# DeltaNet and mixture of depths on one core: TensorE filler products, two of six block inversions on GpSimd, the others in PSUM, `y` in one bank

## The chip, the cores and the metric

The kernel runs on one core of a Trainium2 chip. The time is the device time of one execution in microseconds (us); lower is better. Three runs of the kernel before took 437.75, 440.28 and 440.36 us, median 440.28.

Five engines work in their own instruction order and wait for one another through semaphores: TensorE (PE in the profile; PEld is its weight loading), VectorE (DVE), ScalarE (ACT), GpSimd (POOL) and SyncE (SP), which here only issues DMAs. SBUF is the working memory with 128 partitions, PSUM the memory into which TensorE writes.

## The reference

Two parts follow each other. The first is a DeltaNet recurrence over 768 tokens for 4 batches of 8 heads with head size 48; the second picks 128 of 768 tokens of each batch by a score, sends them through a two-layer MLP and adds the gated result.

```python
k_n = k / (np.linalg.norm(k, axis=-1, keepdims=True) + 1e-06)
for t in range(S):
    y[:, :, t] = np.einsum('bhd,bhde->bhe', q[:, :, t], state)
    v_old = np.einsum('bhde,bhd->bhe', state, kt)
    state = state + bt[:, :, :, None] * np.einsum('bhd,bhe->bhde', kt, vt - v_old)
...
scores = np.einsum('bsd,d->bs', x, w_gate)     # x is y with the heads side by side
for b in range(B):
    top_idx = np.argpartition(-scores[b], capacity)[:capacity]
    xe = x[b, top_idx]
    ye = np.maximum(xe @ w1, 0.0) @ w2
    out[b, top_idx] = x[b, top_idx] + g[:, None] * ye      # g: sigmoid of the score
```

## The kernel before

**Units and blocks.** The recurrence is done in chunks of 64 tokens. Two batches with all their heads (16 sequences) make a group, and a chunk of a group is a unit: 2 groups x 12 chunks = 24 units, `i` = 0 to 23, each group's 12 one after the other because the state passes from chunk to chunk. Within a chunk the tokens depend on each other through a triangular 64x64 system. The kernel inverts its two 32x32 diagonal halves directly and joins them with products. Four units make a block, `e` = 0 to 5, whose 32x32 triangles stand side by side on VectorE's 128 partitions.

**Preparation (`prep`, L383).** For each unit SP loads `k` and `q`; TensorE transposes them (L335) into PSUM banks of the ring `inv`, ScalarE copies them to `kq` (L339); TensorE forms `k k` and `k q` products (L352), ScalarE copies them to `g` and `p` (L361); GpSimd masks `p` with two selects (L369); two DMAs in SP's queue shift half of `g` to other columns (L380).

**Elimination (`eliminate`, L418).** Once per block on VectorE: transpose `g` into `a` (L423), norms and scales (L433 to L438; the root on ScalarE), GpSimd makes the table `mb` (L441), scale (L448), then 30 steps of two instructions each. Step `j` multiplies column `j` of the rows below with row `j` into `tmp` (L458) and subtracts that from the rows below (L462), so that (31 - j) x j elements per partition are worked on twice; both operands are in SBUF. Then the table (L468) and two transposes back (L471 into `tt`, L476 into `g`); SP moves half of `tt` (L482).

**Join (`join`, L500).** For each unit two sets of 32 small 32x32 products (L514, L525) with ScalarE's copies between (L519, L530). The first set waits for L471.

**Recurrence (`recur`, L540).** For each unit a chain: products of `k` with the state (L562), VectorE's subtraction from `v` (L566), products with the inverse (L574), two copies on ScalarE (L580), the update of the state in PSUM (L588, weights from `k`), a copy of it (L594), and on to the next unit. Beside the chain stand VectorE's scaling of `v` (L554) and the output `y`: products of `q` with the state (L601) and of `p` (L611). Two units share a PSUM tile `py` of two banks, each writing one half of its partitions. Every second unit ScalarE copies `y` to `x` (L618), SP stores it (L626), VectorE forms the score (L632).

**Depths (`depths`, L677).** For each of 4 batches: the scores are spread over all partitions (L687 on GpSimd, L697 on TensorE), VectorE counts each token's rank (L729, L734), makes the selection (L742), TensorE turns it into indices (L749), GpSimd gathers 128 rows (L764), TensorE runs the MLP (L770, L780, L794), ScalarE gates (L799), GpSimd adds the rows to the output (L803).

**Order of the work.** All instructions are written out by a planner (`Plan`, L26). Each piece of work has an engine, a reckoned duration, dependences and a due time (`prio`, lower first). The planner runs through time, always takes the piece that can start first, on equal start the lower due time, and emits them in order of their planned starts; every engine works through its own list in that order. Rings (`ring`, L202) are sets of buffers; a piece that takes one waits in the plan until one is free. `k` has 10 buffers, `kq` and `p` have 9 each, so nine units can be prepared ahead, `g` and `tt` have 2 (blocks), `inv` has 3 PSUM banks, `y` one tile of two banks, and `prec` and `psta` take the other three banks.

## Time and profile before

| | us |
|---|---|
| median of 3 runs | 440.28 |
| the profiled execution | 440.75 |
| its span, first to last instruction | 439.0 |
| TensorE busy (PE) | 325.6 |
| VectorE busy | 279.6 |
| ScalarE busy | 154.5 |
| GpSimd busy | 65.0 |
| mean granted clock of TensorE | 0.754 |

[...] "Busy" for TensorE is the time in which at least one matmul was under way. An engine that waits is listed with the instruction that released it. A duration stands for one instruction unless a count (x32) follows; then it is the time of all of them together.

### The profile page before, as it was taken

Reading aid. Unit: us, or ns where it says so; the run is one execution under the profiler, and the core shown is the slowest. Engines: PE = TensorE matmul, PEld = TensorE weight load, DVE = VectorE, ACT = ScalarE, POOL = GpSimd, SP = SyncE. Lnnn points to the kernel's source line nnn. Section 1 sums busy time; section 2 is a strip of 40 time slices with the busy share of each in tenths; the row PEclk is TensorE's granted clock in tenths of the full one; section 3 lists DMA queues with packets and bytes.
Section 4 is the critical chain, followed back from the end, with each engine's and each line's share of the span. In section 5 each row is a group of like instructions: output and inputs, shape, how many; then the busy total and the mean of one; then the engine's idle time right before and its main releaser. Section 6 shows DMA issues by size and latency. Waiting matters only on the chain. (4 is left out here: it accounts for less than half of the span.)

```text
span 439.0 us, 13687 instructions
## 1 busy us (share of the span) xinstructions
PE 325.6 (74%) x5884; PEld 282.2 (64%) x5884; DVE 279.6 (64%) x741; ACT 154.5 (35%) x381; POOL 65.0 (15%) x84
## 2 busy tenths in 40 slices
PE   2749508996999849996999608999429999339383
PEld 2637308994898749875898408997329997128281
DVE  3029999689748997699655998469995110984000
ACT  0545405346534633546423605342016141201010
POOL 3025212014011212023010310100100001100201
PEclk9965755798559965998559955599855699757869
DMA  9545764355325541354223202222111011100201
GB/s 124 106 86 102 143 187 106 60 121 92 82 37 116 111 81 31 84 108 88 55 40 75 37 6 45 55 56 38 19 25 40 19 40 18 37 18 1 35 1 18
DMA packets 108444, 27.92 MB, mean 64 GB/s; under 512 B 103072, under 2 KB 107808, under 8 KB 108384
## 3 DMA queue, kind: packets, MB, share of 16 engines
q1 hardware_dynamic: 103184, 24.67, 27.0%
q0 software_dynamic: 832, 1.57, 2.2%
q10 hardware_dynamic: 4368, 0.80, 1.3%
q8 instruction: 46, 0.75, 0.7%
q14 instruction: 14, 0.11, 0.1%
HBM read 18.38 MB, written 5.51 MB: 54 GB/s over the span
## 5 line engine op out<-in xcount | busy, mean ns | idle before, releaser
L458 DVE TENSOR_TENSOR tmp<-a 128x30 f32<-128x30 f32 (+9 forms) x180 | 67.6, 376 | 5.6
L462 DVE TENSOR_TENSOR a<-a,tmp 128x30 f32<-128x30 f32 (+9 forms) x180 | 66.1, 367 | 6.2
L514 PE MATMUL inv<-tt,g 32*32 32x32 f32 x768 | 22.8, 235 | 52.2 <-DVE tt L471 52.2
L369 POOL TENSOR_SCALAR_AFFINE_SELECT p<-p 64x512 f32<-64x512 f32 x48 | 36.0, 751 | 144.0 <-ACT p L361 142.7
L514 PEld LDWEIGHTS inv<-tt,g 32*32 32x32 f32 x768 | 21.3, 150 | 55.8 <-issue 28.4
L611 PE MATMUL py<-wbd,p 128*64 128x96 f32 x384 | 44.6, 280 | 0.0
L352 PE MATMUL inv<-kq 48*64 48x128 f32 (+1 forms) x896 | 36.5, 293 | 7.8 <-ACT p L361 4.6
L580 ACT COPY wbd<-prec 64x384 f32<-64x384 f32 x48 | 22.7, 473 | 55.7 <-PE prec L574 50.4
L611 PEld LDWEIGHTS py<-wbd,p 128*64 128x64 f32 x384 | 40.2, 161 | 2.5 <-issue 1.4
L566 DVE TENSOR_TENSOR r<-v,prec 128x384 f32<-128x384 f32 x22 | 12.2, 554 | 41.6 <-PE prec L562 41.5
L519 ACT COPY g<-inv 32x256 f32<-32x256 f32 x48 | 17.4, 362 | 59.7 <-PE inv L514 44.4
L352 PEld LDWEIGHTS inv<-kq 48*64 48x64 f32 x896 | 28.0, 158 | 14.0 <-ACT p L361 6.3
L729 DVE TENSOR_SCALAR_CACHE_REDUCE junk<-rep,own 128x256 bf16<-128x256 f32 (+4 forms) x60 | 31.8, 530 | 2.0
L574 PE MATMUL prec<-r,tt 64*64 64x48 f32 x704 | 32.7, 253 | 0.0
L574 PEld LDWEIGHTS prec<-r,tt 64*64 64x64 f32 x704 | 29.6, 168 | 1.5 <-issue 0.6
L339 ACT COPY kq<-inv 128x512 f32<-128x512 f32 x48 | 27.1, 601 | 9.2 <-PE inv L335 9.1
L601 PE MATMUL py<-s,kq 48*64 48x48 f32 x704 | 30.1, 235 | 0.0
L780 PE MATMUL inv<-xeT,w_sb 128*128 128x128 f32 x192 | 28.4, 313 | 1.2 <-ACT xeT L774 1.2
L335 PE MATMUL inv<-ident,k 128*128 128x128 f32 x96 | 18.3, 324 | 14.0 <-DMA k<-in_k_dram 6.6
L601 PEld LDWEIGHTS py<-s,kq 48*64 48x64 f32 x704 | 26.6, 150 | 2.7 <-issue 1.3
L780 PEld LDWEIGHTS inv<-xeT,w_sb 128*128 128x128 f32 x192 | 26.6, 224 | 2.6 <-ACT xeT L774 2.0
L632 DVE SCALAR_TENSOR_TENSOR junk<-x,wg 128x384 bf16<-128x384 f32 x24 | 13.6, 568 | 22.3 <-ACT x L618 21.6
(78 smaller groups left out, 480.8 us busy)
## 6 DMA issues: line engine op xcount, KB each, us to landing
v<-in_v_dram SPq DMA_DIRECT2D x48, 96.0 KB
out_dram<-x SPq DMA_DIRECT2D x24, 192.0 KB
k<-in_k_dram SPq DMA_DIRECT2D x44, 96.0 KB
q<-in_q_dram SPq DMA_DIRECT2D x44, 96.0 KB
g<-g SPq DMA_DIRECT2D x48, 32.0 KB
w_sb<-in_moe_w_dram SPq DMA_DIRECT2D x3, 512.0 KB
w_sb<-in_moe_w_dram SPq DMA_DIRECT2D x4, 384.0 KB
tt<-tt SPq DMA_DIRECT2D x12, 128.0 KB
```

Source lines behind the costliest of these rows:

```text
L339: nc.scalar.copy(got("kq", i)[:, :, o], got("inv", i, nm).rearrange("p (r t) -> p r t", t=P))
L352: nc.tensor.matmul(bank(i, w, rt)[half[par], r, o], lhsT=kq[ds[rt], r, 0, half[par]], rhs=kq[ds[rt], r, o, half[par]], start=True, stop=True)
L369: nc.gpsimd.affine_select(out=t[half[par]], in_=t[half[par]], pattern=[[0, GP], [1, C]], base=0, channel_multiplier=-1, compare_op=ALU.is_ ...
L458: nc.vector.tensor_tensor(out=t, op=ALU.mult, in0=a[:, j + 1:, j:j + 1].to_broadcast([P, w, j]), in1=a[:, j:j + 1, :j].to_broadcast([P, w, ...
L462: nc.vector.tensor_tensor(out=a[:, j + 1:, :j], in0=a[:, j + 1:, :j], in1=t, op=ALU.subtract)
L514: nc.tensor.matmul(ps[lo[par], b], lhsT=g[hi[par], n0 + b, :HC], rhs=tt[hi[par], n0 + b, HC:], start=True, stop=True)
L574: nc.tensor.matmul(pw[half[par], a % 2, a // 2], lhsT=tt[half[par], ch * GP + a], rhs=x[half[par], a], start=True, stop=True)
L580: nc.scalar.copy(wb[half[par], :, par].rearrange("p (r b) d -> p b r d", b=2), pw[half[par]])
L601: nc.tensor.matmul(y[rows, rt, (2 * a + par) * D:(2 * a + par + 1) * D], lhsT=kq[ds[rt], a, 1, half[par]], rhs=s_old[ds[rt], a, par], star ...
L611: nc.tensor.matmul(y[rows, a % 2, (a // 2) * 2 * D:(a // 2 + 1) * 2 * D], lhsT=t[:, a], rhs=wb[:, a].rearrange("p h d -> p (h d)"), start= ...
L729: nc.vector.tensor_scalar(out=junk[:, :(y - x) * P], in0=rows[:, x * P:y * P], scalar1=mine, scalar2=None, op0=op, op1=ALU.add, accum_out= ...
L780: nc.tensor.matmul(got("inv", b, "h", f // 2)[:, f % 2 * CAP:(f % 2 + 1) * CAP], lhsT=w1_sb[:, t, f * P:(f + 1) * P], rhs=got("xeT", b)[:, ...
```

## The change

1. **Fillers.** Whenever the plan lets TensorE idle for about 0.7 us or more, it puts in products whose results nobody reads: 128 x 128 weights, 256 columns moving, bf16, one for every 0.45 us of planned idle time, into the `inv` bank that comes free first.
2. **Blocks 1 and 3 on GpSimd.** Their 30 steps run there, in SBUF as before; transposes, scales and the end stay on VectorE. Their due times are lowered, and so are those of their units' preparation; the table `mb` comes behind the steps.
3. **Blocks 0, 2, 4, 5 in PSUM.** ScalarE copies `a` into a PSUM tile `A` (two banks); the steps read their row from there and subtract there; the multiplied column still comes from `a` in SBUF, `tmp` stays in SBUF.
4. **`y` in one bank.** It loses its two banks to `A` and takes one bank of the ring `inv` per unit; even and odd heads write different halves of the partitions (columns of TensorE's array), so products that follow each other alternate between them. ScalarE copies and SP stores after each unit, four smaller DMAs instead of two every second unit; GpSimd multiplies `x` by the gate's weights (`weigh`), ScalarE sums (two accumulating passes); the last unit's score stays on VectorE. Scores and their diagonal select now have 64 tokens a column.
5. **Buffers and queues.** `kq` and `p` hold 12 units and two more (units 10 and 11) in the space of `w1`, which is loaded later; block 2's `g` lies in the space of `w2`. `k` has 3 buffers, and the state update reads a second copy, `ks`, loaded again (22 units). The shift of the first four units goes to ScalarE's queue, the other units' shifts are done two units at a time. `beta` of block 0 is loaded through GpSimd's queue, a first root runs on ScalarE at the start, and some constants are ordered otherwise.

```diff
+    def fill(self, start, end, done):
+        slots = self.rings["inv"]
+        k = min(range(len(slots)), key=lambda x: slots[x])
+        t = max(start, slots[k]) + 0.1
+        while t + 0.6 < end:
+            op = Op()
+            op.eng, op.start, op.end, op.take, op.give, op.seq = "PE", t, t + 0.25, k, [], -1
+            self.fills.append(op)
+            t += 0.45
...
             at, op = best
+            if op.eng == "PE":
+                self.fill(free["PE"], at, done)
...
+    SPARE = (10, 11)
+    POOL_E = (1, 3)
...
-    ring("k", 10, [GP, DP])
+    ring("k", 3, [GP, DP])
+    ring("ks", 4, [GP, D])
...
-    ring("kq", 9, [GI, 2, P])
-    ring("p", 9, [GP, C])
+    ring("kq", 12, [GI, 2, P])
+    ring("p", 12, [GP, C])
...
-    ring("x", 2, [DM])
+    ring("x", 2, [GB, DM // 2])
+    ring("xw", 1, [GB, DM // 2])
...
-    rings["y"] = [psum.tile([P, 2, 512], FP32, name="py")]
-    plan.ring("y", 1)
+    rings["A"] = [psum.tile([P, HC, HC], FP32, name="pa")]
+    plan.ring("A", 1)
...
-    N["beta", 0] = act(2.6, lambda: load_beta(nc.scalar, 0), prio=-35, lat=2.5)
+        load_beta(nc.gpsimd, 0)
...
-        u = 40 * (e - 1) + 2 * (i % BC)
+        u = 40 * (e - 1) + 2 * (i % BC) - 40 * (e in POOL_E)
...
-        n["mp"] = pool(1.4, mask_p(i), [n["e", 1, 0], n["e", 1, 1]], u + 20)
-        n["sh"] = sp(1.3, shift(i), [n["e", 0, 0], n["e", 0, 1]], u, lat=2.5)
+        n["mp"] = pool(1.4, mask_p(i), [n["e", 1, 0], n["e", 1, 1]], 10 * i - 10)
+        done = [n["e", 0, 0], n["e", 0, 1]]
+        if first:
+            n["sh"] = act(1.3, shift(i, 1, nc.scalar), done, u, lat=2.5)
+        elif i % 2:
+            n["sh"] = sp(1.3, shift(i, 2, nc.sync), done +
+                         [N[i - 1]["e", 0, 0], N[i - 1]["e", 0, 1]], u - 5, lat=2.5)
...
     def eliminate(e):
-        u = 40 * (e - 1) + 8
+        on_pool = e in POOL_E
+        u = 40 * (e - 1) + 8 - 60 * on_pool
+        eng, run = (nc.gpsimd, pool) if on_pool else (nc.vector, dve)
...
+        def fill():
+            nc.scalar.copy(got("A", e), got("a", e))
...
                 a = got("a", e)
+                x = a if on_pool else got("A", e)
+                t = tm[:, :w * j].rearrange("p (i c) -> p i c", c=j)
+                eng.tensor_tensor(
                     out=t, op=ALU.mult,
                     in0=a[:, j + 1:, j:j + 1].to_broadcast([P, w, j]),
+                    in1=x[:, j:j + 1, :j].to_broadcast([P, w, j]))
+                eng.tensor_tensor(out=x[:, j + 1:, :j], in0=x[:, j + 1:, :j],
+                                  in1=t, op=ALU.subtract)
+            return emit, (0.55 + 4.2e-3 * w * j if on_pool else 0.38 + 2.08e-3 * w * j)
...
         last = dve(1.4, scale, [s["sc"]], u)
+        if not on_pool:
+            last = act(1.1, fill, [last], u - 500, take=[("A", e)])
         for j in range(1, HC - 1):
             emit, dur = step(j)
-            last = dve(dur, emit, [last], u)
+            last = run(dur, emit, [last], u + 1000 * on_pool)
+        if on_pool:
+            s["mb"] = pool(1.3, table, [last], u, take=[("mb", e)])
...
-        yk = ("y", i // 2)
-        rows = half[c % 2]
+        yk = ("inv", i, "y")
...
         def mm_s():
-            t = got("k", i)
+            t = got("ks", i)
...
-                            y[rows, rt, (2 * a + par) * D:(2 * a + par + 1) * D],
+                            y[half[rt], (2 * a + par) * D:(2 * a + par + 1) * D],
...
-                    y[rows, a % 2, (a // 2) * 2 * D:(a // 2 + 1) * 2 * D], lhsT=t[:, a],
+                    y[half[a % 2], (a // 2) * 2 * D:(a // 2 + 1) * 2 * D], lhsT=t[:, a],
...
         def put(bb):
             def emit():
-                nc.sync.dma_start(out=out[g * GB + bb, (c - 1) * C:(c + 1) * C, :],
-                                  in_=got("x", i, bb))
+                dst = out[g * GB + bb, c * C:(c + 1) * C, :].rearrange(
+                    "t (r b e) -> b t r e", b=2, e=2 * D)
+                for rt in range(2):
+                    nc.sync.dma_start(out=dst[rt], in_=got("x", i)[half[rt], bb]
+                                      .rearrange("p (r e) -> p r e", e=2 * D))
+            return emit
+
+        def weigh():
+            nc.gpsimd.tensor_tensor(out=got("xw", i), in0=got("x", i), op=ALU.mult,
+                                    in1=wg[:, None, :].to_broadcast([P, GB, DM // 2]))
...
+    def filler(m):
+        nc.tensor.matmul(rings["inv"][m][:, :256], lhsT=warm[:, :P], rhs=warm, start=True, stop=True)
```

## Rows read from the trace of the kernel before

**Rows 1.** The page, busy us, share of the span and instructions of each engine.

```profile
PE 325.6 (74%) x5884; PEld 282.2 (64%) x5884; DVE 279.6 (64%) x741; ACT 154.5 (35%) x381; POOL 65.0 (15%) x84
```

**Rows 2.** Waits: us in total, times, longest us.

```profile
PE inv L514 <- DVE tt L471: 52.2, 6, 13.7
```

**Rows 3.** Windows: stretch, length, busy PE, PEld, DVE, ACT, POOL, clock, DMA, GB/s.

```profile
0.00:67.00 67.00, 31.98 (x465) 25.73 (x467) 38.61 (x94) 22.50 (x53) 16.35 (x31) 0.74 0.66 129
67.00:372.60 305.60, 257.83 (x5259) 228.45 (x5254) 215.77 (x548) 123.74 (x308) 41.96 (x46) 0.76 0.28 59
```

**Rows 4.** Windows of 2 us around one gap, same columns.

```profile
250.00:252.00 2.00, 1.10 (x32) 0.86 (x32) 1.86 (x5) 0.78 (x4) 0.67 (x1) 1.00 0.17 26
...
254.00:256.00 2.00, 0.00 (x0) 0.00 (x0) 1.86 (x5) 0.00 (x0) 0.36 (x1) 0.50 0.10 16
...
286.00:288.00 2.00, 2.00 (x47) 1.78 (x45) 0.00 (x0) 0.00 (x0) 0.00 (x0) 0.61 0.00 0
```

**Rows 5.** Windows of the six cold stretches: the fifth, and their sum.

```profile
264.00:286.00 22.00, 21.23 (x438) 19.95 (x439) 13.80 (x46) 10.84 (x26) 1.18 (x1) 0.50 0.21 50
...
sum 116.00, PE 112.34 PEld 104.91 DVE 74.92 ACT 54.95 POOL 12.38; mean PE 18.72 PEld 17.49 DVE 12.49 ACT 9.16 POOL 2.06
```

**Rows 6.** Timeline 322:372, TensorE: start us, us, engine, line, operation.

```profile
339.77 1.95 PE L574 MATMUL prec<-r,tt 64*64 64x48 f32 x32
...
350.79 1.14 PE L574 MATMUL prec<-r,tt 64*64 64x48 f32 x32
...
368.50 1.53 PE L611 MATMUL py<-wbd,p 128*64 128x96 f32 x16
```

**Rows 7.** Window 176:202 (full clock), TensorE: L588, then L335, then L352.

```profile
176.00:202.00 26.00, 1.74 (x32) 1.33 (x32) 1.00 0.46 97
...
176.00:202.00 26.00, 4.97 (x32) 3.45 (x32) 1.00 0.46 97
...
176.00:202.00 26.00, 5.42 (x128) 3.97 (x128) 1.00 0.46 97
```

**Rows 8.** Groups by line and form: GpSimd's selects of two sizes.

```profile
L687 POOL TENSOR_SCALAR_AFFINE_SELECT sel<-tok 128x512 f32<-128x512 f32 x4 | 2.5, 637 | 36.8 <-PE inv L749 27.9 <-DVE junk L632 6.2 <-PE inv L697 2.6
...
L687 POOL TENSOR_SCALAR_AFFINE_SELECT sel<-tok 128x256 f32<-128x256 f32 x4 | 1.6, 406 | 8.0 <-DVE junk L632 3.9 <-PE inv L697 2.3 <-DVE junk L729 1.8
```

**Rows 9.** Durations of L566, L554 and L369: ns min/median/max.

```profile
L566 DVE TENSOR_TENSOR r<-v,prec x22: 553/554/555, 79.1 to 356.1; 128x384 f32<-128x384 f32 x22
...
L554 DVE TENSOR_TENSOR v<-v,nnT x24: 545/556/1639, 34.1 to 308.0; 128x384 f32<-128x384 f32 x24
...
L369 POOL TENSOR_SCALAR_AFFINE_SELECT p<-p x48: 651/674/1677, 24.6 to 253.7; 64x512 f32<-64x512 f32 x48
```

**Rows 10.** Timeline 48:84, VectorE and GpSimd.

```profile
62.95 0.19 DVE L458 TENSOR_TENSOR tmp<-a 128x30 f32<-128x30 f32 x1
...
72.04 2.25 POOL L441 TENSOR_SCALAR_AFFINE_SELECT mb<-bh 128x1024 f32<-128x1024 f32 x1 [15.93 <-DVE nnT L438]
...
73.24 1.07 DVE L458 TENSOR_TENSOR tmp<-a 128x30 f32<-128x30 f32 x1
```

**Rows 11.** Timeline 366:440, TensorE's products with 2 and 384 columns.

```profile
408.34 1.40 PE L749 MATMUL inv<-tok,sel 128*128 128x2 f32 x12
...
426.98 5.33 PE L794 MATMUL inv<-w_sb,hT 128*128 128x384 f32 x16
```

**Rows 12.** Timeline 0:48, the first shifts and the first block.

```profile
17.02 8.11 SPq L380 DMA_DIRECT2D g<-g  x6
...
29.55 1.90 DVE L423 STREAM_TRANSPOSE a<-g 128x1024 f32<-128x1024 f32 x1 [24.47 <-DMA g<-g]
```

**Rows 13.** SP's queue: an issue's duration; largest and smallest of its waits.

```profile
L324 SPq DMA_DIRECT2D v<-in_v_dram x48: 595/627/1534, 14.2 to 305.2; - x48
...
SPq L626 <- ACT x L618: 46.1, 12, 17.9
...
SPq L380 <- ACT rep L704: 0.2, 1, 0.2
```

More of the change, by code (lines that the diff above doesn't have):

```diff
@@ L81, in pick @@
         return min(fits or urgent, key=lambda c: (c[1].prio, c[1].seq))
+    def fill(self, start, end, done):
[7 more added lines that the diff above has]
+            t += 0.45
     def order(self):
-        free, ready, last, done = {}, {}, {}, []
+        free, ready, last, done, self.fills = {}, {}, {}, [], []
         for op in self.ops:
@@ L120, in order, with emit @@
             done.append(op)
-        return sorted(done, key=lambda o: (o.start, o.seq))
-    def emit(self):
+        return sorted(done + self.fills, key=lambda o: (o.start, o.seq))
+    def emit(self, filler):
         left = dict(self.refs)
         for op in self.order():
+            if op.seq < 0:
+                filler(op.take)
+                continue
             for _, key in op.take:
@@ L258 @@
     tok = [sbuf(f"tok{b}", [NT, 2]) for b in range(B)]
-    wg = sbuf("wg", [DM])
+    wg = sbuf("wg", [DM // 2])
+    fold = sbuf("fold", [C])
+    warm = sbuf("warm", [256], BF16)
     w1_sb = sbuf("w1_sb", [KD, F])
     w2_sb = sbuf("w2_sb", [KF, DM])
+    spare = w1_sb.rearrange("p t f -> p (t f)")
+    w = GI * 2 * P
+    rings["kq2"] = [spare[:, m * w:(m + 1) * w].rearrange("p (r o t) -> p r o t", o=2, t=P)
+                    for m in range(2)]
+    plan.ring("kq2", 2)
+    w = GP * C
+    rings["p2"] = [spare[:, 4 * w + m * w:4 * w + (m + 1) * w]
+                   .rearrange("p (r t) -> p r t", t=C) for m in range(2)]
+    plan.ring("p2", 2)
+    rings["g2"] = [w2_sb.rearrange("p f d -> p (f d)")[:, :NB * C]
+                   .rearrange("p (n t) -> p n t", t=C)]
+    plan.ring("g2", 1)
     nrm = sbuf("nrm", [2, HC])
@@ L264 @@
     bh = [sbuf(f"bh{m}", [HC]) for m in range(2)]
-    tmp = sbuf("tmp", [HC * HC // 4])
+    tmp = [sbuf(f"tmp{m}", [HC * HC // 4]) for m in range(2)]
     rhs = [sbuf(f"r{m}", [GP, D]) for m in range(2)]
@@ L269 @@
     junk = sbuf("junk", [S], BF16)
-    own = [sbuf(f"own{b}", [NT]) for b in range(2)]
+    sc = [sbuf(f"sc{b}", [NCH]) for b in range(B)]
     count = [sbuf(f"count{b}", [NT, 4]) for b in range(2)]
@@ L280, in constants @@
         nc.vector.memset(psta, 0.0)
+        nc.vector.memset(ones, 1.0)
+        load_beta(nc.gpsimd, 0)
         for t in wbd:
@@ L679, in depths @@
         g, bb = divmod(b, GB)
-        score = tok[b][:, :, 1]
-        ow, cnt = own[bb], count[bb]
+        own, cnt = tok[b][:, :, 1], count[bb]
         stages = ((0, 4), (4, NT))
@@ L710, in emit @@
             def emit():
-                nc.tensor.matmul(got("inv", b, "own", j0)[:, :j1 - j0], lhsT=ident,
-                                 rhs=score[:, j0:j1], start=True, stop=True)
+                for h in range(2):
+                    nc.tensor.matmul(got("inv", b, "own", j0)[half[h], :j1 - j0], lhsT=fold,
+                                     rhs=sc[b][:, 2 * j0 + h:2 * j1:2], start=True, stop=True)
             return emit
@@ L810, in depths @@
             w = j1 - j0
-            sc = [N["score", b, j] for j in range(j0, j1)]
+            ss = [N["score", b, x] for x in range(2 * j0, 2 * j1)]
             free = N.get(("ranked", b - GB))
-            dg = pool(0.3 + 0.13 * w, diag(j0, j1), sc, u, take=[("sel", b, j0)] + [("rep", b)] * (j0 == 0))
+            dg = pool(0.5 + 0.2 * w, diag(j0, j1), ss, u, take=[("sel", b, j0)] + [("rep", b)] * (j0 == 0))
             mr = pe(0.22 * w, spread(j0, j1), [dg], u, take=[("inv", b, "rep", j0)],
@@ L817, in depths @@
                      give=[("inv", b, "rep", j0)])
-            mo = pe(0.15, mm_own(j0, j1), sc, u, take=[("inv", b, "own", j0)])
-            eo = dve(0.2, out_own(j0, j1), [mo, free], u, give=[("inv", b, "own", j0)])
+            mo = pe(0.15, mm_own(j0, j1), ss, u, take=[("inv", b, "own", j0)])
+            eo = dve(0.2, out_own(j0, j1), [mo], u, give=[("inv", b, "own", j0)])
             for j in range(j1):
@@ L835, in depths @@
         N["gather", b] = ga = pool(
-            1.6, gather, [xi] + [N["put", b, j] for j in range(NT)], u,
+            1.6, gather, [xi] + [N["put", b, x] for x in range(NCH)], u,
             take=[("xe", b)], lat=3.5)
```

175 lines of the change are left out of this document (96 added, 79 removed).

## The prediction

> **What bounds the kernel now.** I read the page first. TensorE is busy for 325.6 us of 439.0 and VectorE for 279.6, so neither fills the span, while GpSimd works for 65.0 [rows 1]. The waits say how the two take turns: TensorE's first join product (L514) waits 52.2 us in six times for VectorE's block (L471) [rows 2]. Then I cut the span at the first join product (67.0) and behind the last product of `y` (372.6). The middle is 305.6 us long with TensorE busy for 257.8; the 66.4 us behind it are ranking and two MoE batches one behind the other [rows 3].
>
> The middle repeats six times, once for each block: TensorE runs dry while VectorE eliminates, then works without a break. [...] Six such cold stretches, 116 us together, hold 112.3 us of TensorE work at 0.50 [rows 5]. They are full of work, so their length is on the path. The kernel is bound in turn by VectorE's block (the gaps) and by TensorE, often at half clock.
>
> **The parts.** All sums are made against the profiled execution: 439.0 us of span and 1.75 us around it, 440.75; the median of the runs is 440.28, so 0.5 us is no matter. A measurement of this kernel tells about 1% from no change.
>
> *Start (67.0 us before).* Removed: the shift of the first four units in SP's queue, where six of its DMAs take 8.1 us of queue because they stand behind loads and waits; they move to ScalarE's queue. The first block began at 29.55, after 24.5 us of idle that this DMA ended [rows 12]. Added: only three `k` buffers, so loads wait for transposes, and units 4 to 7 have the same due times as 0 to 3 and go between them; block 1's transposes and scales stand ahead of block 0's steps on VectorE, because its due time is lower. Both ends by rows: minus 8 (the six shifts' whole queue time) and plus 8 (four more transposes such as the 1.90 us one ahead of it, for what is put between). I take -4: 63.
>
> *The cold clock.* Fillers are bf16 products over the whole array, put where the plan sees TensorE idle for 0.7 us or more, one for every 0.45 us. If they hold the clock through every gap, the 112.3 us of cold work shrink as L574's 32 products do, from 1.95 to 1.14 us [rows 6], a factor of 0.585: 46.6 us are won. Nothing paces a filler: in the real gap all run at its beginning. What one costs has no row; the nearest are the f32 products with a moving side of 2 columns, 1.40/12 = 0.12 us, and of 384, 5.33/16 = 0.33 us [rows 11], so 0.12 to 0.33, and I take 0.2, which covers less than half of a gap. The long gaps can still go cold, the short ones not. I take 60% of the gain, -28; the ends are 0 and -46.6.
>
> *Alternating column tiles.* L611's 16 products took 1.53 us at full clock, all into one half of the columns [rows 6]. L588 has the same 128 rows and 96 columns moving, and alternates: 1.74 us for 32, 0.87 for 16 [rows 7]. L611 should come to that: 0.66 x 24 = -16. The ends are 0 and -24 (the same ratio at half clock). It is off the chain of the state, but in a middle that TensorE fills it counts in full.
>
> *Preparation moved ahead.* `kq` and `p` hold 12 + 2 units instead of 9, so five more are prepared while block 0 is on VectorE. At full clock a unit's share of the four in 176:202 is 4.97/4 + 5.42/4 = 2.6 us [rows 7]: -13 from the middle. The start has room: TensorE is busy for 32 of its 67 us [rows 3]. The ends are 0 (loads come too late) and -13.
>
> *Fillers ahead of ready work.* The plan's gaps are not the chip's. I take 50 fillers that delay real work by 0.2 us, +10; the ends are 0 and 25 (75 of them at 0.33).
>
> *Two blocks on GpSimd.* Each has 30 steps of two instructions over 2 x 4960 = 9920 elements per partition. No row shows GpSimd with two inputs. With one, 512 elements take 637 ns and 256 take 406 [rows 8]: 0.90 ns an element and 0.175 us fixed. Low end, as if the second input were free: 60 x 0.175 + 9920 x 0.9 ns = 19 us. For two inputs I double the slope, and the fixed part too since each waits for the one before: 60 x 0.35 + 9920 x 1.8 ns = 39 us, the value I take. High end: the slope doubled once more, 57 us. [...]
> Is it in time? Block 1 starts at about 38 (an estimate: 8 us behind block 0's 29.55), GpSimd has 28 mask instructions of 0.674 us [rows 9] to put in, 19 us, and some 8 us for table, transposes and join follow: unit 4 can begin at 65 + 39 = 104. With a middle of about 233 us, 9.7 a unit, TensorE gets there at 65 + 39 = 104. Block 3 starts at 96, with 20 masks (13.5 us) and nine weighings of 0.9 us (384 elements at 1.8 ns and 0.175): unit 12 can begin at 86 + 2 x 39 = 164, TensorE comes at 181. So block 1 is just in time and block 3 early; I put +6 for lateness.
>
> *VectorE's blocks in PSUM.* In the trace a VectorE step with two SBUF inputs stands still behind GpSimd: 128x30 took 1.07 us beside GpSimd's table, which itself took 2.25, and 0.19 alone [rows 10]. L566 with one input in PSUM took 553 to 555 ns in all 22 cases, L554 with both in SBUF 545 to 1639 [rows 9]. So PSUM should free the steps of blocks 0 and 2 from GpSimd's long work. [...]
> Does a step cost more in PSUM? By the medians of 554 and 556 ns, no [rows 9]; the copy into PSUM adds one 128x1024 pass on ScalarE, 1 to 2 us a block. [...] Either way VectorE has slack: four blocks instead of six.
>
> *`y` in the `inv` ring, new queues.* `y` now takes one of three banks from its first product to its copy, where it had its own. Before, 305.6 - 257.8 = 47.8 us of the middle were idle, nearly all in the waits for VectorE [rows 2, 3], and those go. What is late next is a bank, ScalarE (two score passes and a copy more for a unit) or a link of the chain. I take 8% of 200 us, +16; the ends are 0 and 48, the idle time of before. SP has more to issue, a rival below.
>
> *Tail.* The same operations; the halved diagonal adds under 1 us, warm products save about that. 66.4 stays.
>
> Sum of the middle: 257.8 - 28 - 16 - 13 = 200.8 busy, + 10 + 6 + 16 = 232.8. Whole: 63 + 232.8 + 66.4 + 1.75 = **364 us**.
>
> **Rivals.**
> *All covers hold.* The clock never falls (18.6 more won), GpSimd is in time (6), half of the stalls don't come (4 to 8): 335. For it: the gaps are VectorE's [rows 2], and a third of its blocks leave it. Against: once the clock is down, the small products behind a gap ran 22 us without lifting it [rows 5].
> *The fillers don't keep the clock.* They run out early in each gap and only cost their time: 364 + 28 = 392. For it: they are not paced, and 0.50 is there soon after the last product [rows 4]. Against: the gaps become shorter, as two blocks leave VectorE.
> *GpSimd late.* At 57 us unit 4 begins at 122 and unit 12 at 200, both 18 to 19 later than TensorE could; block 3 is late through block 1 and not again: 364 + 18 = 382. It would be slower than before only from about 85 us a block (86 + 2 x 85 + 12 x 9.7 + 66.4 + 1.75 = 441).
> *SP's queue becomes the bound: slower.* Puts go from 24 to 96, `k` is loaded a second time (44 more), shifts fall from 48 to 20: by the loops 248 issues become 337. At 0.627 us each [rows 13] the 247 that remain behind the start are 155 us of the middle. SP also waits at its head, in order: 224.5 us in 32 groups before (L891 and L900, the frame, left out), the largest for `x` [rows 13]. If 170 us of it stays and stands ahead of loads, the middle is 325 and the whole 63 + 325 + 66.4 + 1.75 = 456. It decides from 309 us of middle, 154 us of waiting. Against it: most of that waiting had nothing urgent behind it.
>
> **How the numbers follow.** Forecast (350 to 378): 0.37. All covers hold: 0.20. Fillers don't keep the clock: 0.20. GpSimd late: 0.15. SP: 0.08. The range goes from 332, under the best case, to 408, over the cold clock and some of GpSimd's lateness together; outside I leave SP's case, extremes of both and some of the stalls. Likeliest case alone: 350 to 378. Faster by over 1%: 0.89, all of the first four but a little; slower: 0.08, SP; within 1%: 0.03.
>
> **What would show it.** Right: L514's waits for L471 fall to under 15 us; the granted clock stays at 1.00 from the first join to the last unit but for one or two stretches; L611's 16 products near 0.9 us; VectorE's steps at the durations of before while GpSimd works; GpSimd's 60 instructions near 39 us. Wrong: a join that waits for GpSimd's last step (GpSimd late); 0.50 in TensorE's full stretches (no cover); TensorE idle behind DMA loads with SP never idle (SP); a first join later than 72 (start); TensorE under 85% busy with waits for banks. A time over 408 would mean that a new wait took the place of VectorE's.

## The result, and the profile after

| | before | after |
|---|---|---|
| median of the runs | 439.68 us (437.75 to 440.36, 4 runs) | 410.90 us (404.79 to 411.94, 4 runs) |
| profiled execution | 440.75 | 409.91, span 408.1 |
| ratio | 1 | 0.927, 95% interval 0.916 to 0.938 |

The change is faster by 7%, and the prediction was too hopeful: 364 us, with a range up to 408. Set beside the forecast, the profiled execution is 46 us too long: 13.0 in the start, 33.7 in the middle, -0.8 in the tail. This chapter is about these 46 us.

The page's first part, which answers to [rows 1]. GpSimd now works for 154 us instead of 65, and VectorE for 218 instead of 280:

```profile
PE 323.1 (79%) x5969; PEld 270.1 (66%) x5969; DVE 218.1 (53%) x573; ACT 179.0 (44%) x477; POOL 154.3 (38%) x239
```

The three stages, cut as before at the first join product (now L587) and behind the last product of `y` (now L683). Columns: stretch, length, busy time of each engine (instructions), TensorE's granted clock as a share of full speed, DMA share, GB/s; they answer to [rows 3]:

```profile
0.00:76.00 76.00, 55.34 (x655) 42.10 (x655) 39.60 (x99) 32.96 (x81) 32.73 (x61) 0.89 0.68 116
76.00:342.50 266.50, 220.14 (x5061) 191.27 (x5061) 155.52 (x378) 136.38 (x372) 110.59 (x168) 0.76 0.39 82
342.50:408.10 65.60, 47.60 (x255) 36.71 (x254) 23.02 (x99) 9.63 (x25) 10.97 (x12) 0.82 0.12 22
```

In the middle TensorE's busy time fell by 37.7 us, from 257.8 to 220.1, and its idle time hardly at all: 47.8 before, 46.4 now. Its mean clock there is 0.76, as it was.

The waits of the first join product, which answer to [rows 2]: 52.2 us before, 18.6 now. By the last releaser only 5.6 are for a block's transpose (L537), but 9.4 of the other 13.0 had passed when the last block's transpose ended, as its timeline further down shows:

```profile
PE inv L587 <- DVE tok L801: 13.0, 1, 13.0
PE inv L587 <- DVE tt L537: 5.6, 2, 3.1
```

The stretches of the middle at 0.50, cut along the granted clock (TensorE alone); they answer to [rows 5]. Three of seven are shown, and the sum over all:

```profile
118.50:156.00 37.50, 30.93 (x681) 0.50 0.44 82
...
258.00:275.50 17.50, 16.60 (x380) 0.51 0.28 51
299.00:333.50 34.50, 22.87 (x516) 0.51 0.11 22
sum 130.50, PE 107.10; mean PE 15.30
```

The six stretches of [rows 5] leave out their edges, 112.3 us of work. Taken whole, as the seven here are (67.0 to 82.5, 107 to 130.5, 158 to 175, 205.5 to 229, 253.5 to 286.5, 315 to 349), they hold 117.9 in the kernel before:

```profile
sum 146.50, PE 117.93; mean PE 19.65
```

So 107.1 us of work were done at 0.50, against 117.9. Little of the clock was won back. One reason stands in the place of the fillers. Of 69 only 23 ran in the middle, 31 in the start and 15 in the tail, by windows of their line (stretch, length, busy time, clock, DMA share, GB/s):

```profile
76.00:342.50 266.50, 4.91 (x23) 0.76 0.39 82
```

The last gap, which is empty from 298 to 310, had none of them.

Groups of TensorE's instructions in the middle (operations, then busy time and mean ns). L611 of before had 44.6 us there; its successor L683 has 23.5, and 2.4 more in a second group. The two MoE groups (L864, L878) had 12.6 and 11.1 us of the middle before, for two batches; half of that has moved into the tail, where it is hidden:

```profile
L683 PE MATMUL inv<-wbd,p 128*64 128x96 f32 x352 | 23.5, 288 | 0.0
...
L864 PE MATMUL inv<-xeT,w_sb 128*128 128x128 f32 x48 | 6.2, 283 | 1.0 <-ACT p L414 1.0
L878 PE MATMUL inv<-w_sb,hT 128*128 128x384 f32 x16 | 6.0, 506 | 0.0
```

**Where the start went.** Block 0 begins at 30.42, about as before (29.55). Then its square root (L490, ScalarE) waits behind a copy that waits for a transpose, which waits for a load of `q`. The timeline of ScalarE (start, length, line; in brackets the idle time and what ended it):

```profile
37.36 0.59 ACT L392 COPY kq<-inv 128x512 f32<-128x512 f32 x1 [5.07 <-PE inv L388]
37.84 0.23 ACT L490 ACTIVATE nrm<-nrm 128x32 f32<-128x32 f32 x1
```

VectorE idles 5.06 us for it, scales three units' `v` (3.38 us), and starts block 0's steps at 45.5 instead of 37.9. Between them stand block 1's transpose and scales, some 5 us from 54.95 to 60.87. The steps end at 72.7, and the first join comes at 76.0 instead of 67.0.

**Where GpSimd stands.** Its two groups of block steps, between 60 and 206 us:

```profile
L527 POOL TENSOR_TENSOR a<-a,tmp 128x30 f32<-128x30 f32 (+14 forms) x60 | 32.7, 545 | 4.7
L523 POOL TENSOR_TENSOR tmp<-a 128x30 f32<-128x30 f32 (+14 forms) x60 | 29.4, 490 | 4.1
```

Two blocks, 62.1 us of work and 8.8 of idle: 35 us a block. But block 1 ran from 61.4 to 114.0 and block 3 from 141.6 to 204.3, with masks and weighings between the steps. Block 1's product (L533) then came on VectorE behind block 2's, which stood ahead of it in the queue, and its table waited 4.7 us for the one buffer of `mb` that block 2 held:

```profile
120.38 1.23 DVE L533 TENSOR_TENSOR a<-pa,mb 128x1024 f32<-128x1024 f32 x1
121.64 1.94 DVE L537 STREAM_TRANSPOSE tt<-a 128x1024 f32<-128x1024 f32 x1
123.43 1.20 DVE L533 TENSOR_TENSOR a<-a,mb 128x1024 f32<-128x1024 f32 x1
```

**What VectorE did with its freed time: nothing.** From 130 to 190 us, while GpSimd has block 3, VectorE is busy for 13.3 of 60 us (third pair of the row):

```profile
130.00:190.00 60.00, 54.95 (x1346) 49.19 (x1341) 13.27 (x25) 32.77 (x95) 35.75 (x58) 0.73 0.45 100
```

Block 4 wasn't there. Its last two units were prepared at 191 to 197, and their shift stood in SP's queue behind six loads of `k`. Behind the shift came one wait more: ahead of block 4 in VectorE's order stands a selection of the depths (L826), which waited 4.11 us for TensorE, and the block's transpose followed it at once. By how much the selection held it is not shown. The timeline of SP, then of VectorE:

```profile
198.73 4.02 SPq L368 DMA_DIRECT2D k<-in_k_dram  x6
202.84 1.33 SPq L433 DMA_DIRECT2D g<-g  x2
```

```profile
206.95 0.96 DVE L826 TENSOR_TENSOR sel<-iota_r,rank 128x768 f32<-128x768 f32 x1 [4.11 <-PE inv L780]
207.83 1.93 DVE L484 STREAM_TRANSPOSE a<-g 128x1024 f32<-128x1024 f32 x1
...
210.22 1.21 DVE L533 TENSOR_TENSOR a<-a,mb 128x1024 f32<-128x1024 f32 x1
```

The last line is block 3's product: GpSimd had finished its steps at 204.3, but block 4's transpose was ahead in VectorE's queue. So blocks 3 and 4, meant to run side by side, came one behind the other again, and block 5 behind block 4.

### The profile page after: what moved, and what is told of

Its sections match the earlier page's. It is cut to its first block, busy times and chain, and to the rows that moved or that the text cites. A ratio compares the mean times of both kernels' runs of the same rounds, so it can differ in the third digit from the quotient of the medians.

```text
span 408.1 us, 14040 instructions
## 1 busy us (share of the span) xinstructions
PE 323.1 (79%) x5969; PEld 270.1 (66%) x5969; DVE 218.1 (53%) x573; ACT 179.0 (44%) x477; POOL 154.3 (38%) x239
## 5 line engine op out<-in xcount | busy, mean ns | idle before, releaser
L701 POOL TENSOR_TENSOR xw<-x,wg 128x384 f32<-128x384 f32 x23 | 23.5, 1024 | 101.4 <-ACT x L689 99.9
L422 POOL TENSOR_SCALAR_AFFINE_SELECT p<-p 64x512 f32<-64x512 f32 x44 | 31.9, 726 | 43.6 <-ACT p L414 36.9
L523 DVE TENSOR_TENSOR tmp<-a,pa 128x30 f32<-128x30 f32 (+14 forms) x120 | 39.0, 325 | 8.1 <-ACT pa L514 4.7
L527 DVE TENSOR_TENSOR pa<-pa,tmp 128x30 f32<-128x30 f32 (+14 forms) x120 | 40.6, 338 | 4.1
L626 DVE TENSOR_TENSOR v<-v,nnT 128x384 f32<-128x384 f32 x24 | 19.3, 809 | 32.1 <-DMA v<-in_v_dram 32.0
L646 PE MATMUL prec<-r,tt 64*64 64x48 f32 x704 | 32.0, 251 | 4.2 <-ACT tt L603 2.0
L388 PE MATMUL inv<-ident,q 128*128 128x128 f32 x96 | 21.5, 371 | 16.4 <-DMA q<-in_q_dram 11.6
L527 POOL TENSOR_TENSOR a<-a,tmp 128x30 f32<-128x30 f32 (+14 forms) x60 | 32.7, 545 | 4.7
L813 DVE TENSOR_SCALAR_CACHE_REDUCE junk<-rep,tok 128x256 bf16<-128x256 f32 (+4 forms) x60 | 31.7, 528 | 3.5 <-ACT rep L787 1.5
L587 PE MATMUL inv<-tt,g 32*32 32x32 f32 x640 | 18.4, 227 | 18.6 <-DVE tok L801 13.0
L646 PEld LDWEIGHTS prec<-r,tt 64*64 64x64 f32 x704 | 29.0, 166 | 6.0 <-DVE r L638 2.4
L523 POOL TENSOR_TENSOR tmp<-a 128x30 f32<-128x30 f32 (+14 forms) x60 | 29.4, 490 | 4.1
L587 PEld LDWEIGHTS inv<-tt,g 32*32 32x32 f32 x640 | 16.6, 141 | 21.0 <-DVE tok L801 13.1
L388 PEld LDWEIGHTS inv<-ident,q 128*128 128x128 f32 x96 | 15.6, 192 | 20.4 <-DMA q<-in_q_dram 6.0
L864 PE MATMUL inv<-xeT,w_sb 128*128 128x128 f32 x192 | 25.9, 299 | 2.0 <-ACT p L414 1.0
L864 PEld LDWEIGHTS inv<-xeT,w_sb 128*128 128x128 f32 x192 | 24.8, 212 | 3.2 <-ACT xeT L858 1.8
```

Source lines behind the costliest of these rows:

```text
L388: nc.tensor.transpose(ps[:, r * P:(r + 1) * P], x[:, 2 * r:2 * r + 2].rearrange("p b d -> p (b d)"), ident)
L422: nc.gpsimd.affine_select(out=t[half[par]], in_=t[half[par]], pattern=[[0, GP], [1, C]], base=0, channel_multiplier=-1, compare_op=ALU.is_ ...
L523: eng.tensor_tensor(out=t, op=ALU.mult, in0=a[:, j + 1:, j:j + 1].to_broadcast([P, w, j]), in1=x[:, j:j + 1, :j].to_broadcast([P, w, j]))
L527: eng.tensor_tensor(out=x[:, j + 1:, :j], in0=x[:, j + 1:, :j], in1=t, op=ALU.subtract)
L587: nc.tensor.matmul(ps[lo[par], b], lhsT=g[hi[par], n0 + b, :HC], rhs=tt[hi[par], n0 + b, HC:], start=True, stop=True)
L646: nc.tensor.matmul(pw[half[par], a % 2, a // 2], lhsT=tt[half[par], ch * GP + a], rhs=x[half[par], a], start=True, stop=True)
```

## The experiments

Eighteen kernels ran. All ratios are to the kernel before on the same chip; the changed kernel itself, run again beside the fourteenth to sixteenth, had 0.933 (0.927 to 0.938), 409.7 us.

**Is GpSimd's share worth anything?** Edit: `POOL_E = ()`.

> The changed kernel with all six block batches on VectorE (four and two before), everything else as in the change. Theory A (the two blocks on GpSimd pay, as the prediction had it): TensorE waits again for VectorE before each of six blocks, and the time goes back by at least the 20 us that two blocks of 35 us less their transposes are worth, to 430 us or more. Theory B (the division buys nothing, because the first join comes 9 us later through block 1's pieces and blocks 1 to 5 wait for loads and tables anyway): the first join falls from 76.0 to 65 or less, and the time is within 2% of the changed kernel's 411, 403 to 419.

Measured: 417.8 us, 0.943 (0.935 to 0.950). In this run two blocks stood in line for the one buffer of norms, so block 1 took block 2's, and its numbers are not the reference's. The first join came at 68.2 (68.1 in the second run on VectorE alone, below), so most of the 9 us of the start come with block 1's early place. Unit 4's first join came at 116.8 and unit 12's at 205.6, both earlier than with GpSimd (127.9 and 213.6). Theory B was nearer: the division is worth one to two per cent (0.943 beside 0.927 and 0.933), not 20 us.

**Are the fillers worth anything?** Edit: the call of `fill` left out.

> The changed kernel without its 69 filler products; the order of everything else is the same. As predicted (fillers win 28 us of cold clock and cost 10): 411 + 18 = 429 us, with two or three more stretches at 0.50. Rival (they run out at the beginning of a gap and the clock falls in the same places): within 1% of 411, 407 to 415, with the same six cold stretches.

Measured: 413.7 us, 0.933 (0.925 to 0.942), the same as the changed kernel. The work at 0.50 from the first join on (75.2) was 118.5 us instead of 107.1. The rival holds: the 23 fillers of the middle and the 10 just ahead of the first join won at most 11 us of cold work, some 5 us of time by the factor of 0.585, and the 23 were busy for 4.9 us.

**Does the table's buffer hold unit 4?** Edit: `take=[(mk(e), e)]`, with a second tile for block 1.

> Block 1's table on GpSimd gets a buffer of its own (in w2's space, before w2 is loaded), so it no longer waits until block 2 gives the single one back. Theory M (that wait holds unit 4): block 1's last product on VectorE comes within 5 us of its last step on GpSimd (9.4 us in the changed kernel) and ahead of block 2's, the first join of unit 4 comes near 119 instead of 127.9, and the time falls by 6 to 12 us, to 399 to 405. Rival (units 16 to 19 are prepared late for another reason, so that what is won at unit 4 is waited away before unit 16): the join at 119 all the same, but a time within 1%, 407 to 415.

Measured: 414.6 us, 0.940 (0.933 to 0.947). Block 1's product came ahead of block 2's, at 120.0, but behind 58 of block 2's 60 steps, which VectorE's order still puts first; its first join came at 123.3, 4.6 us earlier than in the changed kernel. Both theories were wrong about 119: the buffer held it for these 4.6 us, and the place in VectorE's queue for the rest. The time did not fall, as the rival has it.

**Is SP's queue the bound?** First its length, up. Edit:

```
-                for rt in range(2):
+                for rt in (0, 1) * (2 - bb):
```

> Half of the output writes (those of the first batch of each pair) are issued twice: 48 DMA issues more in SP's queue, 48 x 0.64 = 31 us, nothing else changed. Theory S (SP's in-order queue holds the loads of the later units and so blocks 4 and 5): from 15 to 31 us longer, 426 to 442. Rival (SP's queue has room; it waits 60 us in all in the middle): within 1%, 407 to 415.

Measured: 455.5 us, 1.032 (1.025 to 1.039). Less the changed kernel's 0.933 and times 442 us these are 44 us, 0.9 us for each of 48 issues. Theory S, and more than it asked, though the run doesn't part the issues from the bytes that they write and from the buffers of `x` that they hold longer. Block 4 began at 234.9. Then down, in four ways. Beta's loads on GpSimd at the start:

> The 20 loads of beta for blocks 1 to 5 are issued by GpSimd at its start, where it idles from 7 to 22 us, instead of by SP between the loads of k and q: 20 x 0.64 = 13 us less in SP's queue, all of it before 85 us. Theory S (SP's queue, which issues without a pause to 132 us and again from 138 to 208, sets when a unit is prepared and so when blocks 1, 2 and 4 begin): block 1 begins 3 us and block 4 about 10 us earlier, and the time falls by 8 to 13 us against the changed kernel's 411, to 398 to 403. Rival (GpSimd's blocks and the clock set the middle): within 1%, 407 to 415.

Measured: 409.5 us, 0.934 (0.926 to 0.941), nothing won. Blocks 1 and 4 began at 54.4 and 205.2; in the changed kernel run again they began at 55.2 and 205.3, so these 2.6 us of block 4 are no more than the spread between executions. Half of the writes on ScalarE (`nc.scalar if bb else nc.sync`):

> Of the 96 output writes 48 (the second batch of each pair) are issued by ScalarE, at the same place in the plan's order, instead of by SP: 48 x 0.64 to 0.85 = 31 to 41 us off SP's queue, and 31 us more on ScalarE, which is 44% busy. Theory S, the mirror of the doubled writes (which cost 46 us): 12 to 40 us shorter, 371 to 399, and block 4 begins at 190 or before instead of 207.8. Rival (ScalarE's own in-order queue takes back what SP gives, or SP wasn't the bound): 407 or more.

Measured: 419.2 us, 0.952 (0.941 to 0.962), slower. The rival: between 162 and 192 us a unit's products of `y` came 5 to 7 us behind the last unit's, instead of mostly 3 to 5, and block 4 began at 211.6. But TensorE stood at 0.50 there from 144 to 181.5, in the changed kernel from 118.5 to 156, and 16 products of `y` took 1.55 us instead of 0.88; this run doesn't part ScalarE's longer queue from the clock. Both together:

> Both: beta's loads on GpSimd and half of the writes on ScalarE, 68 of SP's 337 issues. Theory S: the two gains add, 20 to 45 us, 366 to 391. Rival (another bound stands right behind SP's queue: block 3 on GpSimd, or TensorE at 0.50): no more than the better of the two single runs.

Measured: 413.9 us, 0.939 (0.929 to 0.949). And the same with all blocks on VectorE:

> The same relief of SP's queue, but all six block batches on VectorE (with a second buffer for the norms, so that two blocks can stand in line). In the first such pair GpSimd's two blocks were worth 1.5% only (ratios 0.943 and 0.927). Theory S (they were worth little because SP's queue bound both): with SP relieved the pair lies farther apart, this one 15 us or more above the run with both off SP. Rival (they are worth little by themselves): the same 7 us or less.

Measured: 425.3 us, 0.972 (0.965 to 0.979), 11 us above the run beside it. That pair lies farther apart than the first, but this kernel is also slower than the first run on VectorE alone, so the move itself cost it something: no verdict on S from it. What was missing was a relief that costs no other engine. Edit: `range(1 if nm in ("v", "ks") and i > 7 else 2)`, which leaves half of the rows of `v` and of `k`'s second copy out from unit 8 on, so that the numbers are not the reference's.

> From unit 8 on only one half of the rows of v and of k's second copy is loaded (the other half of the products then use what the buffer held before): 31 of SP's issues and their traffic are left out of the middle, nothing is put on another engine, and the order stays. Theory S, the mirror of the doubled writes without ScalarE's extra work: 20 to 30 us shorter, 381 to 391. Rival (SP's queue binds only when it is made longer; other waits stand right behind it): within 1%, 407 to 415.

Measured: 399.8 us, 0.905 (0.898 to 0.911). Blocks 4 and 5 began 6.9 and 8.9 us earlier, which VectorE's timeline of this run shows against 207.8 and 261.4 (205.3 and 260.5 in the changed kernel run again):

```profile
200.98 1.96 DVE L484 STREAM_TRANSPOSE a<-g 128x1024 f32<-128x1024 f32 x1
```

```profile
252.53 1.92 DVE L484 STREAM_TRANSPOSE a<-g 128x1024 f32<-128x1024 f32 x1
```

Some 10 to 12 us for 31 issues and their traffic, half of what S asked. SP's queue with its traffic is one bound of the last blocks: an issue more cost 0.9 us, one less gave back under 0.4.

**Does the early block 1 cost the start?** Edit: `- 40 * (e == 3)` in `prep`.

> Units 4 to 7 are prepared at their own due times instead of with block 0's (the 40 that the change takes off their due time stays for block 3 alone). Theory T (pulling block 1 forward cost the start its 9 us: a load of units 5 to 7 stands ahead of block 0's root on ScalarE through TensorE's transposes, and block 1's pieces stand between block 0's steps on VectorE): the first join comes at 66 to 70 instead of 76.0, and the time falls by 5 to 9 us, 402 to 406. Rival (what the start wins is lost when block 1 is later): the first join at 66 to 70, but a time within 1%, 407 to 415.

Measured: 418.3 us, 0.945 (0.937 to 0.952). The root came at 28.4 instead of 37.8 and the steps began at 39.3, near the 37.9 of before the change; but block 1's transpose and scales still stood between them (55.3 to 62.8), and the first join came at 73.6. Of the 9 us 2.4 came back, and more was lost later. Theory T is right on the root and wrong on the price.

**Can the clock be held?** Fillers where the trace shows TensorE idle, ahead of first joins and of three transposes:

```
+            for _ in range({0: 20, 8: 8, 12: 15, 16: 30, 20: 100}.get(i, 0)):
+                nc.tensor.matmul(got(*key[0])[:, :256], lhsT=warm[:, :P], rhs=warm, ...)
```

> The changed kernel with 282 more fillers, put in TensorE's order where its trace shows it idle: 173 ahead of the first join product of blocks 0, 2, 3, 4 and 5, the others ahead of three transposes that wait for loads. Theory C (the clock is the mis-sized term: 107 us of the middle's work ran at 0.50, nearly as much as the 112 of before): the clock stays at 1.00 behind the gaps at 118, 258 and 299 us, whose 70 us of cold work shrink by a factor of 0.585, so 15 to 29 us shorter, 382 to 396. Rival (behind a gap the chain of products, copies and state sets the pace and not TensorE's rate, or the fillers run out early and the clock falls all the same): within 1% of 411, 407 to 415.

Measured: a median of 422.6 us (415.2 to 426.2 in four runs), beside 442.0 for the kernel before. The 100 fillers ahead of the last join did not run in the gap: they waited 13 us for their bank, and ran behind it. With block 1 at its own time:

> The fillers in the gaps and block 1's own due times together. Theories C and T: 20 to 38 us shorter than the changed kernel, 373 to 391. Rival: no better than the fillers alone.

Measured: 436.3 us, 0.989 (0.983 to 0.996). Who holds the bank stands in the timeline of the changed kernel, VectorE and then TensorE. The copy of the scores (L801) is behind the block's transposes and the ranking, and the join starts when it is done, 3.6 us behind the transpose that it needs:

```profile
304.99 1.90 DVE L537 STREAM_TRANSPOSE tt<-a 128x1024 f32<-128x1024 f32 x1
306.75 2.08 DVE L542 STREAM_TRANSPOSE g<-a 128x1024 f32<-128x1024 f32 x1
...
310.29 0.23 DVE L801 COPY tok<-inv 128x4 f32<-128x4 f32 x2
```

Edit: `nc.scalar.copy(own[...], ...)` at the same place of the order.

> The small copy of the scores out of a bank of the ring (two to a batch, some 0.2 us each) runs on ScalarE instead of VectorE, at the same place of the order. Theory K (a bank of the three is held by a copy that stands behind a block's 60 steps, so the last join comes 3.6 us behind the block's last transpose and the 13 us before it are closed to fillers too): the last join comes within 1 us of the transpose, 3 to 6 us shorter than the changed kernel beside it. Rival (the join waits for the block anyway): within 1% of it, and the join no earlier.

Measured: 408.2 us, 0.927 (0.920 to 0.934). The last join now follows the transpose at once; the time is 0.6% better than that of the changed kernel beside it (0.933), which the intervals don't tell from nothing. Fillers that need no bank, f32 products of `ones` into 64 free columns:

> 245 more fillers as in the run with gap fillers, but f32 products of 64 columns into columns of a bank that nothing else uses, so that they wait for no bank: 150 ahead of first joins (15, 10, 10, 25, 90 for blocks 0, 2, 3, 4, 5), 95 ahead of three transposes that wait for loads. Theory C (the clock is the mis-sized term): the gaps fill, the work at 0.50 in the middle falls from 107 us to under 60, and the time by 12 to 25 us. Rival R (behind a gap the chain of products, copies and state or the next block sets the pace): the cold work falls too, but the time stays within 1% of the changed kernel beside it.

Measured: 450.6 us, 1.015 (1.005 to 1.024). And with the scores' copy on ScalarE:

> Both: the fillers that wait for no bank and the copy of the scores on ScalarE. Theories C and K: 15 to 30 us shorter than the changed kernel beside it, 381 to 396. Rival R: no shorter than the scores' copy alone.

Measured: 445.7 us, 1.004 (0.999 to 1.010). Both were far slower. The 245 fillers, two products each in the trace, were busy for 81.9 us in the first run and 75.6 in the second, more than the 46.4 us that TensorE idles in the changed kernel's middle. But they show something else. The second run's timeline of TensorE has 180 of these products, 90 fillers, without a gap, and its windows the clock beneath:

```profile
300.53 37.67 PE L377 MATMUL prec<-ones 128*128 128x64 f32 x180
```

```profile
306.00:312.00 6.00, 6.00 (x30) 0.50 0.26 44
312.00:318.00 6.00, 6.00 (x30) 0.50 0.00 0
...
```

From 296 to 300 the clock was at 1.00, from 300 to 306 at 0.64 with TensorE busy for 5.80 of the 6 us, and from 306 to 336 at 0.50 with TensorE busy for every one of these 30 us. Last, the change's own bf16 fillers in the gaps, with the bank free:

> The scores' copy on ScalarE, and 146 bf16 fillers of 256 columns in the gaps: 12, 6, 6, 12 and 50 ahead of the first joins of blocks 0, 2, 3, 4 and 5, 38 and 22 ahead of the transposes that wait for loads near 117 and 199 us. Theory C (a clock held through the gap saves 41% of the cold work behind it): the fillers now run inside the gaps, the work at 0.50 in the middle falls from 107 us to 75 or less, and the time by 8 to 15 us against the changed kernel (ratio 0.90 to 0.915). Rival R (the small products of joins and of the first unit let the clock fall again by themselves, and the rest of the gain is lost in waits): cold stretches of 10 us come back behind each join, and the ratio stays at 0.92 to 0.935.

Measured: 405.5 us, 0.917 (0.912 to 0.922): the best version that does all of the work, 1.7% under the changed kernel's 0.933 on another chip, and 1.1% under its first 0.927, whose interval it overlaps. TensorE's timeline at the last gap, then its windows:

```profile
301.61 5.63 PE L587 MATMUL inv<-warm 128*128 128x256 bf16 x50
308.59 1.20 PE L591 MATMUL inv<-tt,g 32*32 32x32 f32 x64 [1.35 <-DVE tt L539]
310.61 1.92 PE L602 MATMUL inv<-g 32*32 32x32 f32 x64 [0.82 <-ACT g L596]
```

```profile
304.00:306.00 2.00, 2.00 (x21) 1.00 0.32 77
306.00:308.00 2.00, 1.24 (x12) 1.00 0.09 21
308.00:310.00 2.00, 1.20 (x64) 1.00 0.07 15
310.00:314.00 4.00, 3.39 (x86) 0.50 0.40 66
...
322.00:326.00 4.00, 3.94 (x71) 0.50 0.02 4
326.00:330.00 4.00, 4.00 (x122) 0.87 0.16 39
```

Here the fillers (L587 in this kernel, the join is L591) did hold the clock through the gap, at 1.00 to the join. At 310 it fell all the same, and stayed down to 327 us. The rows still have 1.35 us of idle time ahead of the join and 0.82 us behind it, so this place alone doesn't tell whether idle time or the small products brought it down; the last run, below, does. The same place in the changed kernel, where the gap was empty:

```profile
298.00:306.00 8.00, 0.00 (x0) 0.57 0.16 37
306.00:310.00 4.00, 0.00 (x0) 0.50 0.39 66
310.00:314.00 4.00, 3.49 (x124) 0.50 0.01 4
...
326.00:330.00 4.00, 4.00 (x83) 0.50 0.07 16
330.00:334.00 4.00, 4.00 (x72) 0.59 0.16 37
```

Behind the empty gap 22.9 us of work ran at 0.50 (the row of 299.00:333.50 above), behind the full one 16.3 (16.27 from 310 to 327): filling the gap took away 6.6 of 22.9. In the whole middle 92.6 us were left at 0.50, of 107.1. Rival R has the mechanism, cold stretches that come back behind the joins; the ratio lies just under its 0.92, and the cold work far above Theory C's 75. The last run moved the writes of units 12 to 23 to GpSimd as well:

> The same, and the 48 writes of units 12 to 23 issued by GpSimd, idle behind its second block, instead of SP: 48 x 0.64 to 0.85 = 31 to 41 us off SP's queue behind 213 us, where it issues nearly without a pause to 252. Theory S (SP's queue holds the last two blocks' preparation): 5 to 12 us shorter than the run before it, as the left-out loads were (10 us). Rival (behind 213 us VectorE's blocks follow one another anyway): the same within 1%.

Measured: 414.5 us, 0.937 (0.930 to 0.943), slower. Block 5's product (L533 of the change) came at 299.7 instead of 305.4, as S says. But TensorE's small products of the ranking, which stand ahead of the fillers and the join, now waited for ScalarE's score passes (idle from 293.8 to 298.4 and from 298.7 to 301.7), so that the fillers began at 302.5, behind the block instead of beside it. ScalarE's timeline has what the first of these passes waited for, and GpSimd's what stood ahead of that: two writes, which had waited for a scatter of the depths, and whose issues took 1.26 us:

```profile
297.84 0.36 ACT L712 ACTIVATE junk<-xw 128x192 bf16<-128x192 f32 x1 [5.29 <-POOL xw L705]
```

```profile
295.53 1.26 POOL L700 DMA_DIRECT2D out_dram<-x  x2 [3.44 <-DMA out_dram<-oe,idx]
296.69 1.12 POOL L705 TENSOR_TENSOR xw<-x,wg 128x384 f32<-128x384 f32 x1
```

For the clock this run is the clean case. Its 50 fillers run straight into the last join, and from 310 to 316 TensorE idles 0.41 us in all. TensorE's timeline, then its windows:

```profile
310.88 1.20 PE L591 MATMUL inv<-tt,g 32*32 32x32 f32 x64
312.42 1.46 PE L602 MATMUL inv<-g 32*32 32x32 f32 x64 [0.34 <-ACT g L596]
```

```profile
310.00:312.00 2.00, 2.00 (x73) 1.00 0.04 8
312.00:314.00 2.00, 1.59 (x74) 1.00 0.00 0
314.00:316.00 2.00, 2.00 (x64) 0.79 0.03 8
316.00:318.00 2.00, 1.87 (x33) 0.50 0.00 0
```

With no gap ahead of it the clock fell between 314 and 316, and stayed down to 332. So it takes no gap for this stretch to run cold.

## Why the prediction was wrong

*The clock*, one of the two largest misses. The forecast took 28 us for it ("I take 60% of the gain"); what came is 10.8 us less work at 0.50 (117.9 to 107.1), by the same factor of 0.585 some 4.5 us: 23.5 missing. Two steps failed. The first is the place of the fillers: they were to cover the middle's gaps, and 23 ran there, none in the last one. The larger is the reading of [rows 4, 5]: I took the gap for the cause of the cold stretch behind it. With fillers in seven gaps 92.6 us of the middle still ran at 0.50, and where they ran up to the last join and the clock was at 1.00, it fell to 0.50 by 316, some 5 us behind the join's start at 310.88. The work behind a gap (32x32 products with copies between them, and the first unit's chain) did not hold the clock in these runs. The sign of it was in [rows 5], a stretch in which TensorE was busy for 21.23 of 22 us and at 0.50, and the prediction used it against one rival only. The run with f32 fillers and the scores' copy has the same sign without a gap: busy for all of the 30 us from 306 to 336, and at 0.50.

*Idle time of the middle.* 22 us were forecast (6 for lateness, 16 for stalls), 46.4 came: 24.4 missing, in several waits, none of them a bank of `y`. The largest are 13.0 us at the last join (9.4 behind VectorE's last block, then 3.6 behind the scores' copy, which held the bank), 14.7 ahead of transposes (5.7 and 4.3 of it for loads), and 6.4 ahead of L646. "VectorE has slack: four blocks instead of six" was the step that failed: slack is no gain for an engine whose next block isn't prepared. The reading of [rows 2, 3] was off as well: the first of the six waits ends at 66.8, in the start, so that of the 47.8 us that were to go 38.7 were waits for VectorE:

```profile
66.79 2.61 PE L514 MATMUL inv<-tt,g 32*32 32x32 f32 x90 [13.58 <-DVE tt L471]
```

After the change block 4 began at 207.8, and from 130 to 190 VectorE was busy for 13.3 of 60 us.

*GpSimd late.* Right on the price, wrong on the clock time. 39 us a block were forecast and 35 measured; the slope was right (128x30 took 0.24 us and 128x240 0.62: 1.8 ns an element), the fixed part 0.19 us, and 0.07 of idle time, instead of 0.35. But block 1's steps began at 61.4, not 38: its transpose came at 54.95 only, among block 0's steps in VectorE's order. And masks and weighings stretched both blocks to 53 and 63 us. Units 4 and 12 began at 127.9 and 213.6 instead of 104 and 164.

*Start.* -4 was forecast, inside -8 to +8; +9 came. The minus was booked for the shifts and came to nothing (block 0 began 0.9 us later), and the plus, block 1's pieces, was seen and given too little. The runs with all blocks on VectorE took 7.8 us of it back.

*Alternating column tiles.* Right: 0.83 to 0.88 us for 16 products at full clock, 0.87 forecast; 44.6 - 25.9 = 18.7 us won, 16 forecast. (The end of -24 doesn't follow from its rows: 0.66 x 24 at half clock is 27, and the same ratio on the 44.6 us is 19.) *Preparation ahead*: 8.4 us won (L352 and L335 had 40.3 us of the middle, their successors 31.9), 13 forecast. *Fillers' cost*: 10 forecast; the 23 of the middle were busy for 4.9, which bounds what they can have delayed. Not foreseen: 11.5 us of MoE products that left the middle for the tail.

*PSUM.* Right. While GpSimd worked on block 1, a step of 128x240 took 0.37 to 0.42 us on VectorE, and 128x30 0.19 to 0.21. No run took the PSUM copy, the column tiles or the earlier preparation out by itself, so these three are read from the two traces alone.

*The sum.* Missing: start 13, clock 23.5, idle time 24.4, preparation 4.6. To the good: MoE 11.5, fillers 5.1, alternation 2.7, tail 0.8. 364 + 65.5 - 20.1 = 409.4; the groups ran at mixed clocks, so that the parts are good to a microsecond or two.

*The rivals.* "The fillers don't keep the clock" (392) named one of the two largest parts. SP's queue was told right as a mechanism that decides once it is made longer (44 us for 48 issues), and wrong as a bound by itself. What stays open is which single queue sets block 4's beginning (SP's, or VectorE's with the selection ahead of it): in the four reliefs of SP it lay between 201.0 and 211.6, against 207.8, and where another engine took the work, the time came out no better.

## What to carry to other kernels

A cold stretch behind a gap is charged to the gap only when a run with the gap filled stays warm: fill one gap first, and look at the clock some microseconds behind it. When work leaves an engine, ask at what time that engine's next piece will be ready, and read it from the queues that prepare it; otherwise the freed time stays empty. In a kernel whose queues all follow one written order, relief on one queue that put work on another was no gain in any of these runs: only leaving work out, and work in a place where its engine truly waits, paid.

## What the hardware showed that was not expected

TensorE's clock fell from 1.00 to 0.50 while 37.67 us of f32 products with 64 moving columns ran without a gap, and stood at 0.50 from 306 to 336 us, whereas bf16 products of 256 columns kept it at 1.00 through the last gap, from 301.61 us to the join at 308.59, in the run that followed. With the small products of the last join it fell between 314 and 316 us of the last run, with 0.41 us of idle time since 310. In the changed kernel's trace an issued DMA took its queue nearly the same on three engines: 0.65 us (median of 8) for the shifts on ScalarE's queue, 2.56 us for four loads of `beta` on GpSimd's, so 0.64 each, and 0.64 (median of 16) for the shifts on SP's. And GpSimd with two inputs in SBUF took 0.24 to 0.26 us for 30 elements and 0.62 to 0.67 for 240, which is 0.19 to 0.20 us and 1.8 to 2.0 ns an element.
